# Mamba-2 SSD and a hard-swish MLP on one core: chunk 0's C load, the order of the opening and the weights' signs

## The chip, the cores and the metric

The kernel runs on one core of a Trainium2 chip. The metric is the device time in microseconds from launch to end, the median of several runs. Times inside a run are told on the clock of the profiled execution: 0 is the start of its span. Engines are PE (TensorE, with PEld for its weight loads), DVE (VectorE), ACT (ScalarE), POOL (GpSimd) and SP (SyncE, which here only issues DMAs); "ACTq" and "SPq" are DMA issues on the queues of ACT and SP.

## What is computed

A state-space scan in chunks, and then a two-layer MLP over all its tokens (the reference's own chunks have 32 tokens; the kernel takes 128, the same mathematics):

```
x: [4, 8, 768, 32]   a: [4, 8, 768]   B, C: [4, 8, 768, 16]
w_in: [256, 2048]    w_out: [2048, 256]        (both float64)

per batch and head, per chunk:
  cum     = cumsum(log a)
  M[i,j]  = (C_i . B_j) * exp(cum_i - cum_j)   for j <= i
  y_i     = sum_j M[i,j] x_j  +  exp(cum_i) * C_i . state
  state   = exp(cum_end) * state + sum_j exp(cum_end - cum_j) B_j x_j^T

X = y as [4 * 768 tokens, 8 * 32]
h = X @ w_in
out = (h * clip(h + 3, 0, 6) / 6) @ w_out
```

[...]

## The kernel before, in words

The 768 tokens are six chunks of 128. Chunk c has 4 batches x 128 tokens = 512 columns; chunk k's MLP is woven with chunk k + 1's scan. The order on every engine is written out by hand (a manual schedule): each engine runs its instructions in the order of the program text, and waits on semaphores for its operands. The order around the change is that of the main body from L969 on.

**Loads.** `load_bc` (L89) loads B and C of a chunk. Chunks 1 and 2 get them with tokens outermost; chunk 0's C, and C and B of chunks 3 to 5, are laid out by pairs of heads in `pairs_first` (L100): eight DMAs of 32 KB each, issued by SP (L104), one for each batch b and parity h, each from a source whose outermost dimension is 4 heads. Each DMA signals one of eight semaphores in turn, so the ninth waits until the first has landed, and so on; the first weights are the first in this round, `a` the second. Chunk 0's C comes after these two (with B, which ACT issues, among them), so that its sixth load waits for the first weights and its eighth for the first load of C. Behind C, SP issues x (L122) and the second part of the weights (L143).

**Weights.** `load_w(i)` (L132) loads one of eight parts of 1 MB: 0 to 3 are quarters of w_in's columns, 4 to 7 quarters of w_out's rows. Three raw buffers are there. `decode(i)` (L195) is a generator that is advanced by `weights(i, n)`, n steps at a time, so that its instructions lie where the main body puts them. Its steps for a part (128 x 1024 elements):

- ACT copies the top 16 bits of each double (L206).
- VectorE builds the significand in two instructions (L209, L213); VectorE cuts the exponent (L223) and the sign (L225) out of the 16 bits.
- ACT turns the exponent into the bits of a bfloat16 power of two by two relus (L229, L231), which also clip.
- VectorE joins the sign to it (L236) and multiplies it with the significand (L249). The result is a quarter of the first layer's weights (`first_in`), or of `w_out`.

**Chunk 0, the opening.** Decays: VectorE and ACT make cum of `a` (L277 to L293, in three bfloat16 parts), PE forms cum_i - cum_j in PSUM (`diff`, in two halves `diff_less` L364 and `diff_pick` L373, over a mask of L352), ACT takes the exponential (`diff_exp` L381). The same products for chunk 1 (`diff(1, ...)`) are also made here. POOL scales B by the decay to the end of a half chunk (`ends`, L412). PE turns B (`turn_b`, L438, copied by ACT at L447). VectorE turns C by 32 x 32 squares (`turn_squares` L481) and masks it by head parity (`part_heads` L488), POOL fades it (`fade` L494). `scores` (L543) is C.B, followed by `into_state` (L555); `multiply` (L585) multiplies decays and scores on VectorE; `mix` (L611) applies them to x and `from_state` (L516) adds the state's part; `keep` (L625) copies y to SBUF on ACT; `renew` (L594, L565) makes the new state. The second part of the scan over `a` (`add_up(ends_at[1])`, L282) feeds two stores by SP (`store_rows`, L299 and L301) and six transposes (`turn_cum` L329) whose result is negated and copied by VectorE (`by_token` L332). `busy` (L506) is a product of the identity with itself that nobody reads.

**First layer of chunk 0.** `mlp_in(0, f)` (L636) for f = 0 to 15: two products of 128 x 512 with f's weights, in four PSUM banks in turn; ACT (L715) and VectorE (L720) empty the bank of f into gT, so f + 4 waits for that. f = 0 to 3 use part 0 of the weights, 4 to 7 part 1, and so on. The steps of parts 2 to 5 are woven between them. The second layer (`first_out`, L735) follows and uses parts 4 to 7. From chunk 1 on the layers are done in another form (L684, L794, L861), with sums of weights and of gT.

Of the kernel before, what the change touches and what calls it, by code (L numbers as in the profile page):

```python
# [21 lines left out]
def kernel(  # L22
# [66 lines left out]
    def load_bc(c):  # L89

        sl = slice(c * P, (c + 1) * P)

        def tokens_first(src, queue=nc.sync, **where):
            t = loads.tile([P, NB * NH, N], FP32, **where)
            queue.dma_start(out=t, in_=src[:, :, sl, :].rearrange("b h s n -> s (b h) n"))
            return t

        def pairs_first(src):  # L100
            t = loads.tile([P, 2, NB, 4, N], FP32, name="pairs", tag="bc")
            for b in range(NB):
                for h in range(2):
                    nc.sync.dma_start(  # L104
                        out=t[:, h, b].rearrange("s a n -> s (a n)"),
                        in_=src[b, h:NH:2, sl, :].rearrange("h (s a) n -> h s (a n)", a=4))
# [25 lines left out]
    def load_w(i, queue=nc.sync):  # L132

        raw = loads.tile([P, NK * FP * 2 * P], U32, name="raw", bufs=NRAW)
        if i < NP:
            cols = slice(2 * i * FP * P, 2 * (i + 1) * FP * P)
            src = moe_w_in[:, cols].rearrange("(k p) f -> p k f", p=P)
            dst = raw.rearrange("p (k f) -> p k f", k=NK)
        else:
            r0 = (i - NP) * FP * P  # L140
            src = moe_w_out[r0:r0 + FP * P, :].rearrange("(k p) m -> p k m", p=P)
            dst = raw.rearrange("p (k m) -> p k m", k=FP)
        queue.dma_start(out=dst, in_=src)  # L143
        raws[i] = raw
# [1 line left out]
    load_w(0, nc.scalar)  # L146
    load_bc(0)
    load_x(0)
    load_w(1)
    nc.scalar.preload_act_table_set("natural_log_exp_and_others")  # L150


# [24 lines left out]
    half_up = const.tile([P, 1], FP32, name="half_up")  # L177
    nc.vector.memset(half_up, UP / 2)
    bias_hi = const.tile([P, 1], FP32, name="bias_hi")
    nc.vector.memset(bias_hi, 1151.0 * 2 ** 7)  # L180
    bias_lo = const.tile([P, 1], FP32, name="bias_lo")
    nc.vector.memset(bias_lo, 255.0 * 2 ** 7)
    head = const.tile([P, NQ, 2], FP32, name="head")
# [11 lines left out]
    def decode(i):  # L195

        n = NK * FP * P  # L200
        top = raws[i].bitcast(U16).rearrange("p (n w) -> p n w", w=4)[:, :, 3]
        lo, hi = (raws[i].rearrange("p (n w) -> p n w", w=2)[:, :, w] for w in range(2))
        se = att.tile([P, 2, n], U16, name="wse")
        s, e = se[:, 0], se[:, 1]
        m = att.tile([P, n], U32, name="wm")
        nc.scalar.copy(out=s, in_=top)  # L206

        def significand():
            nc.vector.tensor_scalar(  # L209
                out=m, in0=hi, scalar1=0xFFFFF, scalar2=0x100000,  # L210
                op0=ALU.bitwise_and, op1=ALU.bitwise_or)
            yield
            nc.vector.scalar_tensor_tensor(  # L213
                out=m.bitcast(FP32), in0=lo, scalar=2.0 ** -32, in1=m, op0=ALU.mult,
                op1=ALU.add)
# [16 lines left out]
        next(parts_m, None)  # L232
# [4 lines left out]
        m, e = m.bitcast(FP32), e.bitcast(BF16)  # L237
        if i < NP:
            if i < 2:
                dst = att.tile([P, NK, FP * P], FP32, name="w32", tag="y", bufs=3)  # L240
            else:
                dst = ffn.tile([P, NK, FP * P], FP32, name="w32", tag=("wide", "back")[i - 2])
            first_in[i] = dst
            m, e = (t.rearrange("p (k f) -> p k f", k=NK) for t in (m, e))
        else:
            dst = w_out[:, (i - NP) * FP:(i - NP + 1) * FP, :]
            m, e = (t.rearrange("p (k f) -> p k f", k=FP) for t in (m, e))
        unit = 2.0 ** -20 if i >= NP else 2.0 ** -20 / Z
        nc.vector.scalar_tensor_tensor(  # L249
            out=dst, in0=m, scalar=unit, in1=e, op0=ALU.mult, op1=ALU.mult)  # L250

# [77 lines left out]
            nc.tensor.transpose(out=c_ps[:, c], in_=cum_c[:, c], identity=ident[:G, :G])  # L329

    def by_token(c_ps):
        nc.vector.tensor_scalar(  # L332
            out=cum_n[:, 2:], in0=c_ps[:, 2:], scalar1=-1.0, scalar2=None, op0=ALU.mult)


    def y_tile(name, dtype):
# [163 lines left out]
        part_heads(c)  # L500
        fade(c)

    def busy(n, bank):

        for _ in range(n):
            nc.tensor.matmul(  # L506
                out=bank.rearrange("p (b i) -> p b i", b=NB), lhsT=ident,
                rhs=ident.unsqueeze(1).to_broadcast([P, NB, P]), start=True, stop=True)

    def from_state(c, a, pairs=range(NQ)):  # L510

        csT, state = bTs[c][2], (mids[c] if a else states[c - 1])
# [501 lines left out]
    renew(0)  # L1014
    weights(1, 1)
    load_eto(1)
# [151 lines left out]
```

## Time and profile before

| What | Value |
|---|---|
| Median of 3 runs | 345.14 us (345.08 to 348.86) |
| The profiled execution's own time | 345.45 us |
| Its span | 343.7 us |
| PE busy | 334.6 us, 97% |
| VectorE busy | 220.1 us, 64% |
| ACT busy | 173.2 us, 50% |
| POOL busy | 142.7 us, 42% |
| First-layer products of chunk 0 start (L636) | 22.98 us |
| They end, second layer of chunk 0 starts (L735) | 50.55 us |
| Chunk 0's C is turned (L481) | 12.63 us |
| Second weights' first pass on ACT (L206) | 18.95 us |

The page gives busy time by engine and, in 40 slices of the span, the busy share in tenths. In a timeline each row has the start, the length (of several instructions merged, from the first start to the last end), the engine, the line, the operation, output and input, and in brackets the idle time of the engine ahead of it with what ended it. The chain of waits is followed back from an end, each piece with start and length. In a table by stretches each row has a stretch, its length, the busy time of the five engines with the number of instructions, the granted TensorE clock, the DMA engines' share and the GB/s that they moved.

### The profile page before, as it was taken

How to read it: one execution, taken by the hardware profiler on the slowest of the kernel's cores; microseconds unless marked ns; L12 is line 12 of the kernel's file. 1: busy time of each engine (PE TensorE's matmuls, PEld its weight loads, DVE VectorE, ACT ScalarE, POOL GpSimd, SP SyncE). 2: the span in 40 equal slices, each digit the busy share in tenths (PEclk: the TensorE clock that was granted, in tenths of full speed). 3: DMA queues.
4: the chain of work that ended last, by engine and by line, in shares of the span. 5: the costliest groups of instructions: out<-in, count | busy, mean ns of one | idle time of the engine just before them, and what ended most of it. 6: DMA issues, size and time to landing. Idle time of an engine off the chain costs nothing.

```text
span 343.7 us, 8181 instructions
## 1 busy us (share of the span) xinstructions
PE 334.6 (97%) x3378; PEld 266.5 (78%) x3378; DVE 220.1 (64%) x357; ACT 173.2 (50%) x359; POOL 142.7 (42%) x139
## 2 busy tenths in 40 slices
PE   6889999999999999999999999999999999999996
PEld 2554448888778888888888888888887788888995
DVE  6689999999698647775438666447666324676011
ACT  4769878738874561564551564561564010565000
POOL 3300000093299923099611199610099400089500
PEclk9999999999999999999999999999999999999999
DMA  8888959206941057242029242051200010200010
GB/s 173 163 341 169 242 187 176 53 2 95 192 61 23 5 69 159 34 60 51 2 34 176 46 56 58 6 64 17 34 13 0 2 19 1 34 12 2 0 33 31
DMA packets 91605, 24.89 MB, mean 72 GB/s; under 512 B 84208, under 2 KB 87952, under 8 KB 91056
## 3 DMA queue, kind: packets, MB, share of 16 engines
q1 hardware_dynamic: 87184, 23.06, 34.8%
q10 hardware_dynamic: 4384, 1.31, 1.7%
q8 instruction: 26, 0.43, 0.5%
q14 instruction: 11, 0.09, 0.1%
HBM read 21.07 MB, written 3.29 MB: 71 GB/s over the span
## 4 chain that ended last, share of the span: by engine, by line
PE 75%; issue 11%; DMA 4%; DVE 2%; ACT 2%; POOL 2%; SPq 2%; POOLq 0%; DVEq 0%
PE h L684 31%; PE wb L861 13%; PE wc L861 8%; PE wa L861 8%; PE oa L794 4%; PE ob L794 4%; PE y L611 2%; PE y L516 2%; DMA raw<-in_moe_w_in_dram 2%; PE cb L543 2%; DMA eto<-cum_e 1%; ACT L L401 1%; POOL bs L412 1%; DMA pairs<-in_C_dram 1%; SPq L321 1%
## 5 line engine op out<-in xcount | busy, mean ns | idle before, releaser
L708 DVE SCALAR_TENSOR_TENSOR gT<-gT,h 128x512 f32<-128x512 f32 x80 | 54.9, 687 | 30.7 <-ACT gT L707 27.9
L707 ACT ACTIVATE gT<-h,half_up 128x512 f32<-128x512 f32 x80 | 55.1, 690 | 33.2 <-PE h L684 33.1
L780 POOL TENSOR_TENSOR s<-gT 128x512 f32<-128x512 f32 x20 | 25.8, 1288 | 66.4 <-DVE gT L708 66.4
L684 PE MATMUL h<-gap,w_gap 128*128 128x512 f32 x160 | 51.8, 409 | 0.0
L684 PE MATMUL h<-high,w_high 128*128 128x512 f32 x160 | 50.7, 398 | 0.1
L684 PE MATMUL h<-low,w_low 128*128 128x512 f32 x160 | 50.3, 395 | 0.0
L700 ACT ACTIVATE h<-h 128x512 f32<-128x512 f32 x40 | 23.5, 588 | 30.4 <-PE h L684 30.4
L684 PEld LDWEIGHTS h<-high,w_high 128*128 128x128 f32 x160 | 29.5, 188 | 8.5 <-DVE h L697 2.1
L684 PEld LDWEIGHTS h<-low,w_low 128*128 128x128 f32 x160 | 30.1, 188 | 7.2
L684 PEld LDWEIGHTS h<-gap,w_gap 128*128 128x128 f32 x160 | 29.9, 188 | 7.1 <-DVE gap L678 0.5
L401 ACT ACTIVATE L<-L,cum_n 128x64 f32<-128x64 f32 x128 | 31.6, 337 | 0.7 <-POOL L L162 0.7
L861 PE MATMUL wb<-s,w_out 128*128 128x256 f32 x128 | 30.7, 382 | 0.0
L419 POOL TENSOR_TENSOR tmp<-state,eto 128x256 f32<-128x256 f32 x5 | 3.6, 721 | 61.0 <-ACT eto L405 60.9
L735 PE MATMUL o<-w_out,gT 128*128 128x256 f32 x128 | 28.7, 381 | 0.0
L697 DVE TENSOR_SCALAR h<-h 128x512 f32<-128x512 f32 x40 | 27.7, 692 | 1.2 <-PE h L684 1.2
L636 PE MATMUL h<-yT,w 128*128 128x512 f32 x64 | 27.7, 594 | 0.0
L780 POOL TENSOR_TENSOR s<-s,gT 128x512 f32<-128x512 f32 x20 | 26.9, 1345 | 1.6
L585 DVE TENSOR_TENSOR L<-L,cb 128x512 f32<-128x512 f32 x24 | 15.3, 682 | 19.1 <-PE cb L543 16.3
L735 PEld LDWEIGHTS o<-w_out,gT 128*128 128x128 f32 x128 | 24.1, 190 | 3.8 <-issue 0.5
L861 PEld LDWEIGHTS wb<-s,w_out 128*128 128x128 f32 x128 | 24.0, 190 | 3.6
L412 POOL TENSOR_TENSOR bs<-B,L 128x128 f32<-128x128 f32 x24 | 13.7, 584 | 30.9 <-ACT L L401 25.8
L780 POOL TENSOR_TENSOR gT<-gT 128x512 f32<-128x512 f32 x20 | 25.9, 1294 | 0.0
(141 smaller groups left out, 534.3 us busy)
## 6 DMA issues: line engine op xcount, KB each, us to landing
raw<-in_moe_w_out_dram SPq DMA_DIRECT2D x4, 1024.0 KB
L<-cum_d SPq DMA_DIRECT2D x8, 512.0 KB
xt<-in_x_dram SPq DMA_DIRECT2D x6, 512.0 KB
raw<-in_moe_w_in_dram SPq DMA_DIRECT2D x3, 1024.0 KB
out_dram<-back SPq DMA_DIRECT2D x128, 16.0 KB
eto<-cum_e SPq DMA_DIRECT2D x20, 64.0 KB
B<-in_B_dram SPq DMA_DIRECT2D x5, 256.0 KB
raw<-in_moe_w_in_dram ACTq DMA_DIRECT2D x1, 1024.0 KB
```

The costliest lines, as they stand in the source:

```text
L401: nc.scalar.activation(Ls[c][:, b, h], Ls[c][:, b, h], AF.Exp, bias=cum_n[:, c, g:g + 1])
L412: nc.gpsimd.tensor_tensor(out=bss[c][:, hs], in0=Bs[c][:, hs], in1=Ls[c][:, b, :, HT - 1:HT].to_broadcast([P, NH, N]), op=ALU.mult)
L636: nc.tensor.matmul(out=h.rearrange("p r i -> p (r i)"), lhsT=first_in[f // FP][:, j, f % FP * P:(f % FP + 1) * P], rhs=yTs[k][:, j], start ...
L684: nc.tensor.matmul(out=h, lhsT=w[:, j, f * P:(f + 1) * P], rhs=y[:, j], start=(start and j == 0), stop=True, skip_group_check=True)
L697: nc.vector.tensor_scalar(out=h, in0=h, scalar1=-Z / UP, scalar2=None, op0=ALU.mult)
L700: nc.scalar.mul(h, h, -Z / UP)
L707: nc.scalar.activation(g, h, AF.Relu, bias=half_up, scale=UP * UP / 6.0)
L708: nc.vector.scalar_tensor_tensor(out=g, in0=g, scalar=UP, in1=h, op0=ALU.min, op1=ALU.mult)
L735: nc.tensor.matmul(out=o[:, b % 2], lhsT=gTs[0][:, f, b * P:(b + 1) * P], rhs=w_out[:, f], start=(f == 0 and b % 2 == 0), stop=True, skip_ ...
L780: nc.gpsimd.tensor_tensor(out=o, in0=p_, in1=q_, op=op)
L794: nc.tensor.matmul(out=bank[:, slot], lhsT=lhs[:, j], rhs=rhs[:, j], start=(clear and j == 0), stop=True, skip_group_check=True)
L861: nc.tensor.matmul(out=bank[:, slot], lhsT=lhs[:, j], rhs=rhs[:, j], start=(clear and j == 0), stop=True, skip_group_check=True)
```

## The change

- `pairs_first` issues one DMA for each pair of heads q and parity h, all batches in it, into 32 partitions; the outermost dimension on both sides is 32 rows.
- In the opening, B is turned and chunk 1's differences 2 and 3 are made before POOL's `ends`; chunk 1's differences 0 and 1 are made one before and one after `scores`; `mix` and `keep` are done by halves with `turn_cum` and `by_token` between them; `by_token` runs on ACT; the two calls of `busy` are gone.
- `load_w(1)` moves from behind x to behind `store_rows`, ahead of `load_w(2)`; `load_w(3)` moves behind `by_token`.
- In `decode`, ACT takes the absolute value of the top 16 bits (read as bfloat16) instead of copying them, so the exponent needs no cutting; the scales and biases of the two relus are changed to fit. For parts 0 to 5 one VectorE instruction takes the sign out of the raw words and joins it (L250 of the changed kernel, `and` then `or`); it replaces three (L223, L225, L236). For parts 6 and 7 ACT makes the sign as a bfloat16 of 1 or -1 (L228) and VectorE multiplies it in (L248). Part 0 joins and multiplies in two halves of its columns.

```diff
@@ load_bc: pairs_first
-            for b in range(NB):
+            for q in range(NQ):
                 for h in range(2):
                     nc.sync.dma_start(
-                        out=t[:, h, b].rearrange("s a n -> s (a n)"),
-                        in_=src[b, h:NH:2, sl, :].rearrange("h (s a) n -> h s (a n)", a=4))
+                        out=t[32 * q:32 * q + 32, h].rearrange("s b a n -> s b (a n)"),
+                        in_=src[:, 2 * q + h, sl, :].rearrange("b (s a) n -> s b (a n)", a=4))
@@
     load_x(0)
-    load_w(1)
@@
-    nc.vector.memset(bias_hi, 1151.0 * 2 ** 7)
+    nc.vector.memset(bias_hi, 1151.0 + 7.5 / 16)
@@ decode
-        nc.scalar.copy(out=s, in_=top)
+        signed = i >= NP + 2
+        nc.scalar.activation(e.bitcast(BF16), top.bitcast(BF16), AF.Abs)
...
-        if i == 0:
+        if i < 2:
             next(parts_m)
             next(parts_m)
         yield
-        nc.vector.tensor_scalar(
-            out=e, in0=s, scalar1=0x7FF0, scalar2=None, op0=ALU.bitwise_and)
-        nc.vector.tensor_scalar(
-            out=s, in0=s, scalar1=0x8000, scalar2=None, op0=ALU.bitwise_and)
+        nc.scalar.activation(e, e, AF.Relu, bias=bias_hi, scale=-1.0 / 16)
         next(parts_m, None)
         yield
-        nc.scalar.activation(e.bitcast(BF16), e, AF.Relu, bias=bias_hi, scale=-8.0)
-        yield
-        nc.scalar.activation(e, e.bitcast(BF16), AF.Relu, bias=bias_lo, scale=-1.0)
+        nc.scalar.activation(e, e, AF.Relu, bias=bias_lo, scale=-128.0)
+        if signed:
+            nc.scalar.activation(s.bitcast(BF16), top.bitcast(BF16), AF.Sign)
         next(parts_m, None)
-        if i and i + NRAW < 2 * NP:
-            load_w(i + NRAW)
-        yield
-        nc.vector.tensor_tensor(out=e, in0=e, in1=s, op=ALU.bitwise_or)
+        yield
...
-        nc.vector.scalar_tensor_tensor(
-            out=dst, in0=m, scalar=unit, in1=e, op0=ALU.mult, op1=ALU.mult)
+        wide = dst.shape[-1]
+        for cols in ((slice(0, wide // 2), slice(wide // 2, wide)) if i == 0 else (slice(0, wide),)):
+            mc, ec, sc, tc_, out_ = (t[:, :, cols] for t in (m, e, s, top, dst))
+            if signed:
+                nc.vector.tensor_tensor(out=ec, in0=ec, in1=sc, op=ALU.mult)
+            else:
+                nc.vector.scalar_tensor_tensor(
+                    out=ec.bitcast(U16), in0=tc_, scalar=0x8000, in1=ec.bitcast(U16),
+                    op0=ALU.bitwise_and, op1=ALU.bitwise_or)
+            if i and i + NRAW < 2 * NP:
+                load_w(i + NRAW)
+            if i:
+                yield
+            nc.vector.scalar_tensor_tensor(
+                out=out_, in0=mc, scalar=unit, in1=ec, op0=ALU.mult, op1=ALU.mult)
@@ by_token
-        nc.vector.tensor_scalar(
-            out=cum_n[:, 2:], in0=c_ps[:, 2:], scalar1=-1.0, scalar2=None, op0=ALU.mult)
+        nc.scalar.mul(cum_n[:, 2:], c_ps[:, 2:], -1.0)
@@ keep
-    def keep(c):
-        yTs[c] = y_tile("yT", FP32)
-        for u in range(2):
-            for a in range(2):
-                nc.scalar.copy(out=y_half(yTs[c], a, u), in_=ys[c][a, u])
+    def keep(c, u):
+        for a in range(2):
+            nc.scalar.copy(out=y_half(yTs[c], a, u), in_=ys[c][a, u])
@@ the main body, opening
     diff(0, 2, 3)
-    weights(0, 1)
+    weights(0, 2)
     for b in range(NB):
         diff_exp(0, b)
     first_eto()
+    turn_b(0)
     diff(1, 2, 3)
-    weights(0, 1)
-    for b in range(NB):
-        ends(0, b)
-    turn_b(0)
-    diff(1, 0, 1)
-    busy(1, ps.tile([P, NB * P], FP32, name="d", tag="f0"))
-    weights(0, 1)
     diff_exp(1, 2)
     diff_exp(1, 3)
     turn_squares(bcs[0][0], turned(0)[2])
     part_heads(0)
-    fade(0, HALF[1], nc.gpsimd)
+    for b in range(NB):
+        ends(0, b)
     add_up(ends_at[1])
     store_rows()
+    load_w(1)
     load_w(2)
     weights(0, 1)
+    diff(1, 0)
+    fade(0, HALF[1], nc.gpsimd)
     scores(0)
+    diff(1, 1)
     multiply(0)
+    yTs[0] = y_tile("yT", FP32)
+    mix(0, (0,))
+    keep(0, 0)
+    c_ps = ps.tile([P, NC, G], FP32, name="c_ps", tag="f3")
+    turn_cum(c_ps)
+    by_token(c_ps)
+    weights(0, 1)
     load_w(3)
-    c_ps = ps.tile([P, NC, G], FP32, name="c_ps", tag="f1")
-    turn_cum(c_ps)
-    busy(1, ps.tile([P, NB * P], FP32, name="d", tag="f0"))
-    weights(0, 1)
-    weights(1, 1)
-    by_token(c_ps)
-    mix(0)
-    keep(0)
-    weights(1, 3)
+    mix(0, (1,))
+    keep(0, 1)
+    weights(1, 4)
     renew(0)
     weights(1, 1)
```

More of the change, by code (lines that the diff above doesn't have):

```diff
@@ L222, in decode @@
         yield
-        nc.vector.tensor_scalar(
-            out=e, in0=s, scalar1=0x7FF0, scalar2=None, op0=ALU.bitwise_and)
-        nc.vector.tensor_scalar(
-            out=s, in0=s, scalar1=0x8000, scalar2=None, op0=ALU.bitwise_and)
+        nc.scalar.activation(e, e, AF.Relu, bias=bias_hi, scale=-1.0 / 16)
         next(parts_m, None)
         yield
-        nc.scalar.activation(e.bitcast(BF16), e, AF.Relu, bias=bias_hi, scale=-8.0)
+        nc.scalar.activation(e, e, AF.Relu, bias=bias_lo, scale=-128.0)
+        if signed:
+            nc.scalar.activation(s.bitcast(BF16), top.bitcast(BF16), AF.Sign)
+        next(parts_m, None)
         yield
-        nc.scalar.activation(e, e.bitcast(BF16), AF.Relu, bias=bias_lo, scale=-1.0)
-        next(parts_m, None)
-        if i and i + NRAW < 2 * NP:
-            load_w(i + NRAW)
-        yield
-        nc.vector.tensor_tensor(out=e, in0=e, in1=s, op=ALU.bitwise_or)
-        m, e = m.bitcast(FP32), e.bitcast(BF16)
+        m, e, s = m.bitcast(FP32), e.bitcast(BF16), s.bitcast(BF16)
         if i < NP:
@@ L243, in decode @@
             first_in[i] = dst
-            m, e = (t.rearrange("p (k f) -> p k f", k=NK) for t in (m, e))
+            parted = NK
         else:
             dst = w_out[:, (i - NP) * FP:(i - NP + 1) * FP, :]
-            m, e = (t.rearrange("p (k f) -> p k f", k=FP) for t in (m, e))
+            parted = FP
+        m, e, s, top = (t.rearrange("p (k f) -> p k f", k=parted) for t in (m, e, s, top))
         unit = 2.0 ** -20 if i >= NP else 2.0 ** -20 / Z
-        nc.vector.scalar_tensor_tensor(
-            out=dst, in0=m, scalar=unit, in1=e, op0=ALU.mult, op1=ALU.mult)
+        wide = dst.shape[-1]
[13 more added lines that the diff above has]
+                out=out_, in0=mc, scalar=unit, in1=ec, op0=ALU.mult, op1=ALU.mult)
     pick = const.tile([P, G], BF16, name="pick")
@@ L501, in turn_all @@
         fade(c)
[L503 to L508, printed above, removed]
     def from_state(c, a, pairs=range(NQ)):
```

## The prediction

> **What bounds the kernel now.** First the page's head and its slices. The span is 343.7 us; the profiled run took 345.45 us, 1.75 more for what lies around it, and the median of the three runs shown is 345.14.
>
> ```profile
> PE   6889999999999999999999999999999999999996
> DVE  6689999999698647775438666447666324676011
> PEclk9999999999999999999999999999999999999999
> DMA  8888959206941057242029242051200010200010
> ```
>
> A slice is 8.6 us. PE is short of full only in the first three slices and the last; asked by stages it is busy 27.57 of the 27.57 us from 22.98 to 50.55, and 255.29 of the 258.7 us after 85. So what can be won lies ahead of 22.98, where the first product of the first layer (L636) starts, and only as far as the products behind it then run without a hole. Next the chain of waits, for the time before that:
>
> ```profile
> 0.80 5.92 DMA raw<-in_moe_w_in_dram
> 6.74 0.61 SPq L104
> 7.40 1.23 SPq L104
> 8.67 3.78 DMA pairs<-in_C_dram
> 12.63 1.18 DVE csT L481
> 14.86 1.25 PE cb L543 x61
> 19.80 0.93 issue
> ```
>
> The reader sees a queue, not an engine: SP's sixth load of C starts when the first weights have landed (6.73), the eighth at 8.67, and its 32 KB take 3.78 us more. VectorE has nothing from 10.29 to 12.63. The stretches by time show how C moves:
>
> ```profile
> 8.00:10.00 2.00, 2.00 (x71) 1.40 (x71) 1.93 (x4) 1.35 (x3) 0.00 (x0) 1.00 0.36 54
> 20.00:23.00 3.00, 2.26 (x101) 1.94 (x101) 2.93 (x6) 1.23 (x4) 0.00 (x0) 1.00 1.04 425
> ```
>
> The last two columns are the DMA engines' share and GB/s: while C is awaited only 0.36 of the 16 engines work, at 54 GB/s; later loads get 425. Last the timelines, for what follows L636 and for single durations:
>
> ```profile
> 18.95 1.17 ACT L206 COPY wse<-raw 128x1024 uint16<-128x1024 uint16 x1 [1.16 <-DMA raw<-in_moe_w_in_dram]
> 26.46 1.23 DVE L249 SCALAR_TENSOR_TENSOR w<-wm,wse 128x1024 f32<-128x1024 f32 x1
> 8.26 1.23 DVE L213 SCALAR_TENSOR_TENSOR wm<-raw,wm 128x1024 f32<-128x1024 uint32 x1
> 2.14 3.57 PE L352 MATMUL d<-hide,ident_h 128*128 128x512 bf16 x8 [2.14 <-POOL head L184]
> 7.56 0.60 PE L364 MATMUL d<-less,split 128*128 128x512 bf16 x2 [1.00 <-DVE split L293]
> 23.39 0.37 SPq L143 DMA_DIRECT2D raw<-in_moe_w_out_dram x1
> ```
>
> The 16 columns f of the first layer take 27.57/16 = 1.72 us each. f = 4 needs the second part of the weights; it is done at 27.69, and PE asks for it at 22.98 + 4 x 1.72 = 29.87. So an earlier start has 2.2 us of slack there, and no more.
>
> **The change, part by part.** Times are on the span's clock.
>
> *C with 32 rows outermost.* Same eight loads of 128 pieces of 256 bytes, same order on SP. The sixth still waits for the first weights, 6.74; the seventh starts at 7.40 and takes between 0.53 (the usual issue of such a load, later chunks) and 1.23; the eighth starts at 8.0 to 8.65. From there its landing took 3.78 with a third of the engines. If all take part there is no backlog, and what remains is a load's latency: the x load issued at 9.27 shows as rising traffic in the half microsecond from 10.5, 1.2 to 1.7 later, and some 0.5 for the end. I take 2.2 (bounds 1.6 and 3.78): C is there at 10.4, bounds 9.6 (VectorE's own work on the first weights ends 9.49) and 12.63. The share of 0.36 is why I lean to the low end. [...] For the C and B of chunks 3 to 5 the same edit is worth nothing: L481 waited for pairs once in the run.
>
> *VectorE behind it.* Transpose to cT takes 1.20, the two cT 0.80, the scan until SP stores 1.23 (12.63, 13.83, 14.63, 15.86). From 10.4: cT ready 12.4, scan done 13.63. The two bit operations of weight part 0 (0.42 and 0.43) are gone from here; they lay in the idle time, worth nothing. ACT takes part 0's first relu (1.15) ahead of the four exponentials, which start at 8.95 instead of 8.57; PE and ACT then finish bT near 12.0, before cT, so that costs nothing unless C is earlier than 9.6.
>
> *PE.* Without the idle products (1.12 each; the first lay in the wait for cT, the second ahead of L611) and with half of chunk 1's differences moved behind the scores, PE is through its earlier products at 12.5: the last of chunk 1's differences ended at 12.87, half a bank pair (0.6) has gone, and the later exponentials free a bank some 0.25 later. Scores start at 12.55 (before 14.86), end 13.75; into_state 0.86, the moved difference 0.6: 15.2. Mix of the first half 0.85 (L585 for its heads ends 15.0), from_state 0.61, c_ps 0.43, second half 0.79, 0.61: 18.5. First-layer products start about 18.6, 4.4 earlier. VectorE's L585 ends 16.2; the joined signs and the product of part 0, by halves, are four times 0.69: first half 17.5, all by 18.9, f = 2 needs it at 22 (L250 and L257 by halves, priced by L585's 0.68 for 512 columns). by_token moves to an idle ACT (0.28). The copies of y end at 19.1.
>
> *Second weights later.* load_w(1) moves on SP from behind x (10.04, held there 4.08, landed 18.95) to behind both stores, and these wait for the scan. Before, SP went from store to next weights in 0.87 (15.86 to 16.73): now 13.63 + 0.87 = 14.5, then load_w(2) at once; load_w(3) waits for part 0's joining, about 18.2 (before 17.3). The w_out load behind it waits for part 1's joining, 24.1 (before 23.39), and what SP has queued after that, chunk 1's decays, C, B and x, comes 0.7 later; POOL asks for the decays at 67.9 and PE for C and B at 66, so 35 us cover it. A megabyte on a drained queue: the w_out load issued at 23.39 shows 240 to 400 GB/s from 25.0 to about 28.2, 4.8 from issue; the first one took 5.92 in company, the one of 17.3 about 7 behind two others. I take 4.8: landed 19.3, 0.35 later than before although all around it is over 2 us earlier. That is now the tight place. Queued behind it: ACT's three passes, 1.15, 1.19 and 1.19 with gaps: 22.85. VectorE: the joined signs. The trace has no such 16-bit operation with a strided input; 0.68 (L236) and 1.23 (L213, same stride in bytes) bound it, I take 1.22: 24.1. Then L594 and L565, 1.0, and the product 1.22: 26.3. Behind these stands the first evacuation, 0.68, which frees f = 4's bank: 27.0. PE itself would be there at 18.6 + 6.89 = 25.5, so it stands 1.5 us at f = 4.
>
> *After that.* VectorE's work per part was 4 x 0.60 + 4.40 = 6.8 against PE's 6.89; it becomes 4 x 0.60 + 4.1 = 6.5. f = 8 asks at 33.9 and gets part 2 at 33.5, f = 12 has 0.8 to spare. Parts 6 and 7 give ACT one pass more each (2 x 1.1), covered by ACT's idle 2.0 before bT (66.73) and the earlier start. From there everything shifts alike.
>
> The sum: 29.87 - 27.0 = 2.9 us. Span 340.8, profiled run 342.55; against the median, which is 0.3 lower, 342.2.
>
> **The rivals.**
>
> *C is no faster.* For it: the sixth load still waits for 6.73, and B's small packets share the engines. Against it: 0.36. Then the transpose stays at 12.63, the weights are issued at 16.73 and land at 21.5, f = 4 at 29.2: 0.7 won, 344.4.
>
> *PE's stop stays.* The 0.93 us at 19.80 waited for nothing the profile shows, while the DMA carried about 400 GB/s. If it falls into the same place of the program, ACT's copies end at 20.0 and hold its first pass: f = 4 at 27.75, 2.1 won, 343.0. Against it: at that place the weights are then only starting.
>
> *Weights in time.* If C lands at 9.6 and the joined signs take 0.68, f = 4 would be free at 25.6, about PE's own 25.5; 4.3 won, 340.8. That is the floor: PE's own chain does not get shorter.
>
> *PE at half speed (slower).* The trace has two speeds: the eight products at 2.14 stand 0.43 apart, the same shape at 7.56 takes 0.60 for two, though PEclk says 1.00 for both. Without the idle products PE could fall back. If all from the scores on (6.0 us to 18.6) ran at half speed, the first layer would start at 24.6 and f = 4 at 31.5: 1.6 lost, 346.8. It decides from 4.4 us lost on PE (1.5 slack and 2.9). Against it: after 7.5 the new order leaves PE fewer holes than the old, which had two of 0.9 and one of 0.6 and kept its speed. [...]
>
> **How the numbers follow.** The forecast's chain 0.55, C no faster 0.13, the stop stays 0.13, weights in time 0.11, half speed 0.05, something unseen 0.03. The likeliest gives 342.2; its own range is 341.4 (C at 9.6) to 343.2 (C a microsecond later than 10.4). With the rivals but the slow one: 340.7 to 344.9. About 2% (6.9 us) is what a measurement of this kernel tells from no change: only half speed for longer, or something unseen, goes beyond it. Faster 0.02, same 0.95, slower 0.03.
>
> **What would show it.** The DMA share between 6.5 and 10 above 1 and the transpose at about 10.4; L636 at about 18.6; the second weights' first ACT pass at about 19.3, waiting for the DMA; a hole of about 1.5 us on PE at f = 4, the wait put down to VectorE, and no further one up to the second layer; the joined signs near 1.22. Wrong it would be if the transpose still starts after 12, if the weights land after 20.5 or before 18, if VectorE falls behind at f = 8, or if products after 7.5 are 0.43 apart in the 16-bit shape.

## The result, and the profile after

The changed kernel takes 349.56 us (median of 18 runs, 346.59 to 351.74), the kernel before beside it 345.45 (18 runs, 344.84 to 348.86). The ratio is 1.0108, 95% interval 1.0085 to 1.0131: some 1.1% slower, within the 2% the prediction named, but on the wrong side and outside its range. The profiled execution took 351.21 us with a span of 349.3, so 1.9 lie around the span (before 1.75). Ratios here are formed without disturbed runs, so they need not equal the quotient of the medians.

Each run also has its mean granted PE clock, and the spans go with it. Of the 18 runs after, 2 have 0.995 (spans 344.7 and 345.7), 9 about 0.990 (346.7 to 348.2) and 7 about 0.985 (348.2 to 349.9); none is at full clock. The profiled run is one of the 0.984. First its slices of 8.7 us:

```profile
span 349.3 us, 8168 instructions
PE   6859999999999999999999999999999999999996
PEclk9967999999999999999999999999999999999999
DMA  9783999601981009234009425014110000200000
```

The row PEclk was 9 throughout before; now its third and fourth slices read 6 and 7, and PE's third slice 5 instead of 8. The loss lies between 17 and 35 us. The chain of waits gives the place:

```profile
7.33 0.43 SPq L104
7.80 3.25 DMA pairs<-in_C_dram
11.23 1.13 DVE csT L488
13.41 1.20 PE cb L543 x59
14.95 0.76 issue
17.87 0.25 PE y L516 x3
18.12 3.89 issue
22.02 1.01 PE y L516 x8
25.74 30.20 PE h L634 x64
```

C is there at 11.23 instead of 12.63, the scores start 1.45 earlier. Then PE stops twice for "issue", a wait for nothing that the profile shows: 0.76 us, and 3.89 us at 18.12, in the middle of one and the same line (3 products of L516 before, 13 after). Behind it the first layer starts at 25.7, not at 22.98, and takes 30.2 us instead of 27.6. The stretches by time say why (last columns: granted clock, DMA engines' share, GB/s):

```profile
0.00:18.13 18.13, 13.39 (x349) 7.64 (x349) 12.96 (x30) 10.49 (x19) 5.79 (x18) 1.00 0.87 147
8.00:10.00 2.00, 2.00 (x69) 1.29 (x67) 1.56 (x2) 1.97 (x4) 0.00 (x0) 1.00 0.96 115
18.00:20.00 2.00, 0.12 (x3) 0.00 (x0) 1.76 (x3) 0.27 (x1) 0.00 (x0) 1.00 0.98 393
20.00:22.00 2.00, 0.00 (x0) 0.00 (x0) 0.14 (x1) 0.00 (x0) 0.00 (x0) 0.64 1.00 403
24.00:26.00 2.00, 2.00 (x65) 1.72 (x50) 0.00 (x0) 0.58 (x2) 0.00 (x0) 0.50 0.61 240
28.00:30.00 2.00, 2.00 (x3) 0.67 (x2) 0.43 (x1) 1.97 (x3) 0.00 (x0) 0.50 0.00 0
30.00:32.00 2.00, 2.00 (x5) 0.91 (x4) 1.96 (x5) 1.25 (x3) 0.00 (x0) 0.80 0.13 9
```

While PE stands, the second and third parts of the weights (asked for at 15.26 and 15.78) pass at 400 GB/s; some 2.5 us after the stop began the clock falls to 0.50 and stays there for about 10 us (0.64 in 20 to 22, 0.80 in 30 to 32), during which first-layer products are twice as long (592 ns at the least, 1222 at the most). From the first layer's end on nothing differs: 293.35 us from there to the end, 293.15 before.

The stop can be counted. The first row above says that PE had run 349 products and 349 weight loads when it stopped; the same count for the kernel before, up to its own unexplained stop of 0.93 us at 19.80:

```profile
0.00:19.81 19.81, 15.12 (x350) 8.12 (x350) 14.00 (x32) 11.32 (x19) 5.80 (x18) 1.00 0.88 194
```

350 and 350. Two programs with a different order stop at the same count, once in the mix and once in L516; with PE's few other records (7 after, 5 before) it is behind the 705th record in both. The smaller stop of after, at 14.95, comes behind the 449th, 256 earlier. And the page has a queue for it (packets, megabytes, share of the engines' time), first for the whole run, then in the DMA view for 19.5 to 19.7 alone:

```profile
q8 instruction: 26, 0.43, 0.5%
```

```profile
q8 instruction: 1, 0.02, 31.2%
```

26 transfers of some 16 KB in the whole run, one of them in the middle of PE's stop, and none that starts from 13 to 19.5. They fit PE alone: 26 pieces of 256 are 6656 instructions, and by the page PE runs 3374 products and 3374 weight loads, VectorE 342 instructions and ScalarE 362. So the theory to test was: PE runs through its small products faster than its instructions come, 256 at a time; the piece behind the 705th record is asked for when PE enters the piece before it (15.71; an inference, since the trace shows when a transfer starts, here 19.6, and not when it was asked for), and here it queues behind the weights asked for from 15.26 on. The rivals: the later second weights cost by coming late ("late data"), or PE lost its clock because the two idle products are gone ("no idle products").

### The profile page after: what moved, and what is told of

Same layout as the page of the kernel before. It is cut to its first block, busy times and chain, and to the rows that moved or that the text cites. A ratio compares the mean times of both kernels' runs of the same rounds, so it can differ in the third digit from the quotient of the medians.

```text
span 349.3 us, 8168 instructions
## 1 busy us (share of the span) xinstructions
PE 337.0 (96%) x3374; PEld 268.4 (77%) x3374; DVE 216.3 (62%) x342; ACT 175.5 (50%) x362; POOL 142.1 (41%) x139
## 4 chain that ended last, share of the span: by engine, by line
PE 92%; DMA 3%; issue 2%; DVE 1%; ACT 1%; SPq 0%; DVEq 0%
PE h L682 31%; PE wb L859 12%; PE h L634 9%; PE wc L859 8%; PE o L733 8%; PE wa L859 8%; PE oa L792 4%; PE ob L792 4%; PE y L611 3%; PE y L516 2%; PE cb L543 2%; DMA raw<-in_moe_w_in_dram 2%; PE y L555 1%; DMA pairs<-in_C_dram 1%; PE t_ps L445 1%
## 5 line engine op out<-in xcount | busy, mean ns | idle before, releaser
L778 POOL TENSOR_TENSOR s<-gT 128x512 f32<-128x512 f32 x20 | 25.8, 1288 | 66.5 <-DVE gT L706 66.5
L634 PE MATMUL h<-yT,w 128*128 128x512 f32 x64 | 30.3, 637 | 0.0
L695 DVE TENSOR_SCALAR h<-h 128x512 f32<-128x512 f32 x40 | 27.6, 691 | 1.2 <-PE h L682 1.2
L634 PEld LDWEIGHTS h<-yT,w 128*128 128x128 f32 x64 | 13.0, 205 | 16.5 <-issue 14.5
```

What stands on the lines that cost most here:

```text
L634: nc.tensor.matmul(out=h.rearrange("p r i -> p (r i)"), lhsT=first_in[f // FP][:, j, f % FP * P:(f % FP + 1) * P], rhs=yTs[k][:, j], start ...
L695: nc.vector.tensor_scalar(out=h, in0=h, scalar1=-Z / UP, scalar2=None, op0=ALU.mult)
L778: nc.gpsimd.tensor_tensor(out=o, in0=p_, in1=q_, op=op)
```

## The experiments

All ran against the kernel before; a table of them stands at the end of this part. Line numbers are those of each kernel, and differ by up to 8 from those of the kernel that it varies. The first four vary the changed kernel.

**e1: the first of the second weights back in its old place.**

```
     load_x(0)
+    load_w(1)
...
     store_rows()
-    load_w(1)
     load_w(2)
```

> The changed kernel with load_w(1) back in its old place behind the x load, nothing else. Theory (the 3.89 us in which PE waits for nothing the profile shows, at its 698th to 705th instruction, is a fetch of its next instructions, held by the two megabytes of weights that are asked for at 15.3 and 15.6; the clock then falls to half for about 10 us): one megabyte less in the way, so the stop shrinks to between 0.9 and 2.5 us at the same count of instructions, the clock stays full from 20 to 30, 343 to 346 us. Rival 'late data' (what costs is that the second weights come later): the stop has nothing to do with the weights and stays at 3.9 us; the time changes by no more than the wait at f = 4, of which the changed kernel has none, so 349 to 350. Rival 'no idle products' (PE without them falls to half speed): half speed from 20 to 30 as before, 347 to 351.

Measured: 350.02 us (349.13 to 350.91), ratio 1.0130 (1.0085 to 1.0176). The stop is still 3.62 us and the clock 0.985 to 0.990. That refutes "late data", since part 1's weights are in time here, but the size of mine missed too. The edit takes less out of the way than I meant: part 1, asked for at 8.64, is still passing when PE enters the piece before at 15.62 (the DMA engines' share is 0.96 from 14 to 16), and part 2 was asked for at 15.19.

**e2: both idle products back.**

```
+    busy(1, ps.tile([P, NB * P], FP32, name="d", tag="f0"))
     scores(0)
...
+    busy(1, ps.tile([P, NB * P], FP32, name="d", tag="f0"))
     mix(0, (0,))
```

> The changed kernel with the two idle products back, one ahead of chunk 0's scores and one ahead of its mix, nothing else. Rival 'no idle products': PE keeps full speed, 344 to 346 us. Theory: the stop is found at the same count of instructions (16 of them are now taken by the idle products, so it lies up to 16 earlier in the program) and is still 3 to 4 us long; half speed for 7 to 10 us behind it; 348 to 351. Rival 'late data': 349 to 351, no difference.

(`busy` is the function of the kernel before. In the trace an idle product is two products and two weight loads, four records and not the eight instructions that I counted.)

Measured: 349.75 us (346.40 to 351.78), ratio 1.0080 (1.0040 to 1.0121). Two of the ten runs are at full clock, the profiled one among them, and in it the stop at the 705th record is 1.34 us; four of the ten have 0.985. The profile puts this stop down to ScalarE's copy of y (L630), but that had ended 0.93 us before. The idle products alone don't bring the time back, against that rival; and the profiled stop isn't 3 to 4 us, against mine: how long the fetch is held is not the same in every kernel that has the weights late. What stop the runs at a lower clock had is not known, since only one run has a profile.

**e3: 64 instructions more, early, in PE's wait for the scan.**

```
+    for _ in range(32):
+        nc.tensor.matmul(
+            out=ds[0, 0][:, 0], lhsT=ident_h, rhs=hide, start=True, stop=True)
     for b in range(2):
         mask_again(0, b)
```

> The changed kernel with 32 small products (64 columns, bf16, 64 instructions with their weight loads) put in at about 6.6 us, where PE waits for the scan, nothing else; they are overwritten. Theory: the stop is a matter of the count of instructions. It is found after 690 to 710 of them again, but 64 earlier in the program: no longer in L516 behind the first half of the mix, but inside the mix, L611. Its length is 1 to 3.9 us, as the fetch before it is asked for about 1.3 us sooner, and still meets the weights. Both rivals and any cause that lies in the data: the stop stays in L516, where a product waits for its operand, and its length stays 3.9. Time by the theory 344 to 350, by the rivals 349 to 350.

Measured: 349.25 us (348.83 to 350.86), ratio 1.0117 (1.0072 to 1.0161). PE's waits (line, what ended the wait, us in all, times, longest), then the counts up to the two stops:

```profile
PE y L516 <- issue: 3.2, 1, 3.2
PE y L611 <- issue: 1.8, 1, 1.8
```

```profile
0.00:16.63 16.63, 13.90 (x349) 8.97 (x350) 11.42 (x28) 10.40 (x18) 5.78 (x18) 1.00 0.92 146
0.00:21.26 21.26, 16.71 (x477) 11.34 (x477) 14.60 (x32) 11.77 (x22) 5.78 (x18) 1.00 0.91 184
```

The stop left its place in L516 behind the first half of the mix and went into the mix itself, L611, 64 instructions earlier in the program and at the same count, 699; and a second stop, which the changed kernel has nowhere, appears 255 instructions later at 954, in the second L516. (With the few other records these are 705 and 961, 256 apart.) What these products read comes from where it came before. The stops belong to the count. This settles what kind of wait it is.

**e4: no weights asked for between 9 and 19.**

```
     load_x(0)
+    load_w(1)
...
     store_rows()
-    load_w(1)
-    load_w(2)
...
     keep(0, 0)
+    load_w(2, nc.scalar)
```

> The changed kernel with load_w(1) in its old place behind the x load, and load_w(2) issued on ScalarE's queue behind the first half's two copies of y, so that no weights are asked for between 10 and about 18.5. Theory: with nothing large in the way the fetch that PE waits for at its 700th instruction takes its quiet time: a stop of 0 to 1 us, full clock throughout, the first product of the first layer at 19 to 20.5, 340.5 to 343.5 us. Rival 'late data': parts 1 and 2 are in time in any case, so it is like e1. Rival 'no idle products': half speed comes back somewhere between 12 and 30, 346 or more.

Measured: 346.82 us (346.15 to 348.41), ratio 1.0044 (1.0019 to 1.0070); two of ten runs at full clock (spans 344.2 and 344.6), three at 0.995, five at 0.990. The stretches of the stop, and the fetch in the DMA answer for 16.8 to 16.9:

```profile
16.00:18.00 2.00, 2.00 (x114) 1.50 (x94) 1.97 (x4) 1.04 (x4) 0.00 (x0) 1.00 0.35 99
18.00:20.00 2.00, 0.85 (x20) 0.70 (x17) 1.97 (x4) 0.34 (x2) 0.00 (x0) 1.00 0.00 0
```

```profile
q8 instruction: 1, 0.02, 60.9%
```

With no weights asked for since 8.70 the fetch starts some 2.8 us earlier, though PE entered the piece before at the same time (15.68, after 15.71), and the stop is 1.15 instead of 3.89; in both PE goes on 2.4 us after the fetch starts. The DMA engines were not at rest yet when PE entered that piece: part 1 was passing until about 16.5 (share 0.91 from 16.0 to 16.5, 0.38 in the next half microsecond). The first layer starts at 21.5. So the mechanism holds, but 340.5 to 343.5 did not come: two stops of 0.74 and 1.15 remain with this order of loads, the clock still falls by a step or two in most runs, and the first layer waits 0.8 and 0.3 us for VectorE.

The next four took two parts of the change alone, on the kernel before, and improved on e4.

**e5: before, without its two idle products.** Edit: the two `busy(1, ...)` lines go.

> The kernel before without its two idle products, nothing else. Theory (PE's small products run faster than their instructions are fetched, 256 at a time; an empty PE then costs granted clock): the stop at the 705th record stays in sight and takes in the second idle product's 1.07 us, so it grows from 0.93 to about 2.0 and the first product of the first layer comes within 0.4 us of 22.98; nothing is won. With two holes of 1.9 and 2.0 us more runs lose one or two steps of clock (0.995, 0.990), 344.5 to 348. Rival 'no idle products' in its strict form (they alone keep the clock): every run has 0.990 or less, 347 to 350. If they are dead weight: 1 us is won, 344.3.

Measured: 350.11 us (349.51 to 351.22), ratio 1.0113 (1.0059 to 1.0167), all four runs at 0.990. PE's waits from 12 to 23:

```profile
PE y L516 <- issue: 2.8, 1, 2.8
PE y L555 <- issue: 0.5, 1, 0.5
```

The strict form of the rival is right here: leaving out two products of 1.07 us whose result nobody reads costs 1.1%. By the trace it is through the same stop: PE reaches the 705th record at 18.91 instead of 19.81, waits 2.8 there, and the first layer starts at 24.9 and at half clock. PE goes on 1.0 later than before (21.7 after 20.7), as it also enters the piece before 0.8 later (16.77 after 15.99, behind the stop of 0.5); in this profile PE's products also ran at a lower rate up to about 11 (see the last section), so it is open how much of that comes from the idle products. I had the place right, the price too low.

**e6: before, with C by heads and nothing else.**

```
-            for b in range(NB):
+            for q in range(NQ):
                 for h in range(2):
                     nc.sync.dma_start(
-                        out=t[:, h, b].rearrange("s a n -> s (a n)"),
-                        in_=src[b, h:NH:2, sl, :].rearrange("h (s a) n -> h s (a n)", a=4))
+                        out=t[32 * q:32 * q + 32, h].rearrange("s b a n -> s b (a n)"),
+                        in_=src[:, 2 * q + h, sl, :].rearrange("b (s a) n -> s b (a n)", a=4))
```

> The kernel before with chunk 0's C loaded by heads, 32 rows outermost, nothing else. Theory: the transpose of C starts at 10.8 to 11.3 instead of 12.63, the scores at 13.9 (PE's earlier products end there) instead of 14.76; the second weights are asked for 1.2 to 1.5 us earlier and meet the fetch for the 705th record, whose stop grows from 0.93 to between 1.5 and 3; the first layer starts between 22.3 and 23.8, 343.5 to 347.5 us, not faster than before by more than 1. Rivals: without that stop 0.8 us are won at once, 344.7.

Measured: 349.32 us (348.33 to 350.48), ratio 1.0096 (1.0071 to 1.0121), clock 0.995 or 0.990 in all ten runs. The chain, and the stretches:

```profile
7.73 0.60 PE d L364 x2
18.29 0.86 PE y L611 x52
19.15 3.04 issue
24.93 7.39 PE h L636 x14
```

```profile
20.00:22.00 2.00, 0.00 (x0) 0.00 (x0) 1.93 (x4) 0.00 (x0) 0.00 (x0) 1.00 0.93 377
24.00:26.00 2.00, 2.00 (x18) 1.37 (x17) 0.00 (x0) 1.32 (x3) 0.00 (x0) 0.50 0.82 255
```

The faster load alone makes the kernel slower by as much as the whole change. It ends VectorE's scan earlier, so SP asks for the third and fourth parts of the weights at 15.10 instead of 16.73, and these now pass ahead of PE's fetch: the stop of before, at the same record and in the same line, grows from 0.93 to 3.04. The time is beyond the 347.5 that I gave as its upper end.

**e7: e4, with the second weights' decode brought forward.**

```
     multiply(0)
+    load_w(2, nc.scalar)
+    weights(0, 1)
+    load_w(3)
+    weights(1, 2)
     yTs[0] = y_tile("yT", FP32)
     mix(0, (0,))
     keep(0, 0)
-    load_w(2, nc.scalar)
...
-    weights(0, 1)
-    load_w(3)
...
-    weights(1, 4)
+    weights(1, 2)
```

> As the run that held the weights back (load_w(1) early, load_w(2) on ScalarE's queue), but load_w(2) right behind the four exponential and state operations, and two of part 1's three ScalarE passes ahead of the copies of y. Theory: the stops stay at about 0.75 and 1.15, the first layer starts at 21.3 to 22, and the two waits of 0.8 and 0.3 us in the first layer are gone; at full clock the span is 342 to 343.3, and most runs have 0.99 to 1.0: 344 to 346 us. If the second weights' earlier request meets the fetch again: a stop of 2 to 3 us and 346 to 349.

Measured: 347.50 us (345.32 to 348.58), ratio 1.0032 (0.9999 to 1.0064). The waits in the first layer are gone, as expected, but one run of ten is at full clock (span 343.6); five have 0.995, four 0.990. So 344 to 346 did not come. In the profiled run, which has 0.995, the longest stop is 1.42 us, with one of 0.2 ahead of it.

**e8: e7 with the two idle products.** Edit: as in e2, on e7.

> As the run beside it (weights held back, part 1 decoded early), with the two idle products back, one ahead of the scores and one ahead of the mix. Theory: PE waits for instructions there in any case (0.64 and 0.75 us around the scores, 1.15 behind the mix), and an idle product is 1.07 us of work in 8 instructions; the stops shrink by what the products fill, so the first layer starts no more than 0.6 us later than without them, and the clock stays at 1.0 in most runs: 343.5 to 345. If the idle products are dead weight: 1 to 2 us longer than without them.

Measured: 344.95 us (344.63 to 345.21), ratio 0.9962 (0.9933 to 0.9991); ten of ten runs at full clock. The chain:

```profile
20.08 0.68 PE y L517 x16
22.52 27.66 PE h L642 x64
```

The idle products delay the first layer by 0.4 us against e7 (22.4 for 22.0) and win 2.5. The stops are 0.34 and 1.06; the second begins at the 705th record, here a wait for a semaphore that ScalarE had raised at 17.3, and the profile puts it down to the next thing that ScalarE ended, a pass that PE reads nothing of. The kernel is faster than the one before by 0.4% (within those 2%), and by the medians 1.3% faster than the changed one.

Of the last four, three go back to the kernel before.

**e9: before, with C by heads and the weights held.** Edit: as in e6, and

```
     store_rows()
-    load_w(2)
...
-    load_w(3)
...
     weights(1, 1)
+    load_w(2, nc.scalar)
+    load_w(3, nc.scalar)
     by_token(c_ps)
```

> The kernel before with chunk 0's C loaded by heads, and load_w(2) and load_w(3) issued on ScalarE's queue behind its first pass of part 1 (about 18 to 20 us) instead of on SP at 15.1; the two idle products stay. Theory (with C alone changed, what cost 3.5 us was that the second weights, asked for at 15.1, met the fetch that PE needs at its 705th record, 3.04 us of stop): the stop shrinks to 0.5 to 1.3, the clock stays at 1.0 in most runs, the first product of the first layer starts at 21.5 to 22.6, and 343.5 to 345 us come out, faster than before by up to 2. Rival (C's new load itself disturbs PE, or an earlier scan does): 347 to 350 as with C alone.

Measured: 344.51 us (344.18 to 345.32), ratio 0.9964 (0.9940 to 0.9987); ten of ten at full clock. No stop is left at the 705th record. The chain, and one stretch:

```profile
7.69 1.03 PE d L364 x2
15.50 1.24 PE cb L543 x59
22.80 27.66 PE h L636 x64
```

```profile
16.00:18.00 2.00, 1.48 (x112) 1.15 (x95) 1.25 (x3) 1.44 (x3) 0.00 (x0) 1.00 0.38 106
```

C's load did no harm by itself: against e6 only two issues have moved (later, and to ScalarE's queue), and by the medians 4.8 us are won. Here the fetch starts at 17.34, 0.7 after PE entered the piece before (16.63), and the weights are asked for only at 17.96. The median is the lowest here.

**e10: before, with only the weights held.** Edit: e9's second part alone.

> The kernel before with load_w(2) and load_w(3) issued on ScalarE's queue behind its first pass of part 1, nothing else. Theory: the stop of 0.93 us at 19.80 was the fetch behind these loads, so it shrinks to 0.5 or less or goes; 344 to 345.5 us, no run or few below a clock of 1.0. Rival: the stop has another cause and stays at 0.93; the time stays, 345.5 to 346.

Measured: 345.59 us (344.84 to 347.18), ratio 0.9993 (0.9964 to 1.0021). The stop of before shrinks as the theory has it; the half microsecond that this is worth can't be told from no change:

```profile
PE y L611 <- issue: 0.5, 1, 0.5
```

What C's load wins on top of it can't be told either: the intervals of e9 and e10 overlap.

**e11: the changed kernel, the stop filled with idle products.** Edit: as in e2, with `busy(4, ...)` ahead of the mix.

> The changed kernel with one idle product back ahead of the scores and four, one behind the other, ahead of the mix (4.3 us of work in 32 instructions), nothing else: PE works while its next instructions are fetched. Theory: the stop falls to under 1 us, since the fetch arrives at about 21 to 22 whatever PE does; the first layer starts at 23 to 24.5, but at full clock: the clock is 1.0 in most runs, 344.5 to 346.5 us, so the price of the stop in the changed kernel was mostly the clock behind it. Rival (the stop is waited out behind the idle products too, or the clock falls for another cause): 349 to 353.

Measured: 349.52 us (348.99 to 349.76), ratio 1.0113 (1.0090 to 1.0136), four of four runs at full clock.

```profile
PE y L618 <- issue: 0.7, 1, 0.7
```

The stop is 0.7 and the clock is kept, both as the theory said, yet nothing is won: PE goes on at 22.87, the first layer starts at 25.5 and waits 0.8 more. So my claim that the stop's price was mostly the clock behind it falls. A late fetch costs its time with the clock kept, too (PE goes on at 19.24 in e4); the clock comes on top where PE stands empty. How much of the delay here is the idle products' own work this run can't tell: PE enters the piece before at 16.2 instead of 15.7 (in this profile its products also ran at a lower rate up to about 11, see the last section), and the fetch starts at 20.6 instead of 19.6.

**e12: before, with the second weights later and nothing else.** Edit: `load_w(1)` from behind `load_x(0)` to behind `store_rows()`.

> The kernel before with load_w(1) moved behind the two stores, nothing else, so that it is asked for at 16.7 with load_w(2); old C, old decode, idle products. Theory: as the scan ends late here, the fetch for the 705th record (asked for at about 16) is ahead of the weights; the stop stays near 0.9 and the clock at 1.0. Part 1 lands at 21 to 22.5, three ScalarE passes and VectorE's part follow, so PE waits 0 to 2.5 us at f = 4: 345 to 348. Rival 'late data' (that the second weights come later is what costs in the change): 347 to 350 here too. If the fetch is held as in the changed kernel: a stop of 2 to 4 and 348 to 351.

Measured: 349.38 us (348.12 to 350.56), ratio 1.0113 (1.0082 to 1.0145), clock 0.995 to 0.989. There is no stop at the 705th record: the scan ends late here, and the fetch was ahead of the weights, as expected (PE entered the piece before at 15.82, the fetch starts at 16.70; the weights were asked for at 16.55). But PE's waits and ScalarE's timeline show another hole:

```profile
PE h L635 <- ACT yT L624: 3.1, 1, 3.1
```

```profile
23.44 1.09 ACT L205 COPY wse<-raw 128x1024 uint16<-128x1024 uint16 x1 [5.83 <-DMA raw<-in_moe_w_in_dram]
24.43 1.19 ACT L624 COPY yT<-y 128x256 f32<-128x256 f32 x4
```

In the order of before, ScalarE's first pass of part 1 stands ahead of the copies of y, so PE waits for the weights through ScalarE. That is the rival "late data" in this order, by a wait I had not seen; the changed kernel has the copies first and is free of it. The clock falls behind this hole as behind the others (0.50 from about 25.8 to 29.2), so what counts is that PE is empty, not why.

**In sum** (times in us; clock steps: runs at 1.000 / 0.995 / 0.990 / 0.985 of the mean granted clock, rounded):

```
kernel                            median  ratio (95%)              PE's hole     first layer  clock steps
changed                           349.56  1.0108 (1.0085, 1.0131)  0.76 + 3.89   25.7         0/2/9/7
 e1 first of second weights back  350.02  1.0130 (1.0085, 1.0176)  0.75 + 3.62   25.3         0/0/3/1
 e2 idle products back            349.75  1.0080 (1.0040, 1.0121)  0.20 + 1.34   22.6         2/3/1/4
 e3 64 instructions more          349.25  1.0117 (1.0072, 1.0161)  1.82 + 3.21   24.7         0/3/1/0
 e4 weights held                  346.82  1.0044 (1.0019, 1.0070)  0.74 + 1.15   21.5         2/3/5/0
 e7 held, decode earlier          347.50  1.0032 (0.9999, 1.0064)  0.19 + 1.42   22.0         1/5/4/0
 e8 e7 + idle products            344.95  0.9962 (0.9933, 0.9991)  0.34 + 1.06   22.4         10/0/0/0
 e11 stop filled                  349.52  1.0113 (1.0090, 1.0136)  0.73          25.5         4/0/0/0
before                            345.45                           0.93          23.0         49/9/5/0
 e5 no idle products              350.11  1.0113 (1.0059, 1.0167)  0.45 + 2.81   24.9         0/0/4/0
 e6 C by heads                    349.32  1.0096 (1.0071, 1.0121)  3.04          24.9         0/4/6/0
 e12 second weights later         349.38  1.0113 (1.0082, 1.0145)  3.13 (ACT)    25.1         0/3/1/0
 e9 C by heads, weights held      344.51  0.9964 (0.9940, 0.9987)  none          22.7         10/0/0/0
 e10 weights held                 345.59  0.9993 (0.9964, 1.0021)  0.45          22.5         9/1/0/0
```

Holes and starts are those of the profiled run, the clock that of all runs (for the kernel before, of its 63 beside e1 to e12). Waits for data of under 1 us are not among the holes.

The traces show the same parts in every stop behind the 705th record: in all twelve profiles that have one, PE goes on 2.2 to 2.8 us after the transfer of 16 KB starts (18.5 in the kernel before, 19.6 in the changed one, 16.8 in e4, 19.4 in e6, 17.9 in e10). What differs is how long that transfer takes to start once PE has entered the piece before: 0.7 and 0.9 us in e9 and e12, where the DMA engines had little or nothing to move, 1.2 in e4, 2.5 in the kernel before, 3.7 to 4.3 in e1, e6, e11 and the changed kernel.

## Why the prediction was wrong, point by point

**What bounds the kernel now** held: all that was lost lies ahead of the first layer and in its first third.

**C** held in kind. The share between 8 and 10 is 0.96 instead of 0.36, so about 15 engines of 16 where it was 6, and 115 GB/s instead of 54, with x in the later figures, which was asked for at 8.28 instead of 9.27. The transpose starts 1.4 us earlier. That all the engines would take part in C was my estimate; the runs show the share of all that passes and not C's own part. My 2.2 for the last landing was 3.25 (the bounds were 1.6 to 3.78), so 11.23 instead of 10.4; the 0.5 for a load's end in it is a term that no run shows.

**VectorE, the weights' signs and their prices** held: the joined signs take 1.23 (forecast 1.22) and 0.68 by halves.

**Second weights later** was mis-sized: asked for at 15.26 (14.5) and, with a second megabyte at once, 6.6 instead of 4.8 to landing, so 21.9 instead of 19.3. It set nothing, since PE was later still: ScalarE began at 26.06, behind its copies of y, and f = 4 never waited for a bank.

**PE: "First-layer products start about 18.6"** is the step that failed. They start at 25.7. Of the 7.1 us, 0.86 come from C, 0.76 and 3.89 from two stops, and some 1.3 from half clock between 22.02 and 25.74 (e4 needs 2.4 us for the same work at full clock, against 3.7); these make 6.8. Another 2.6 were lost in the first layer at half clock. I summed products' durations and had no term for the instructions themselves; but 256 of these instructions take PE about 2.4 us (15.71 to 18.12), and in e4 the next 256 are ready only 3.6 us after PE enters the piece (15.68 to 19.24), in the changed kernel 6.3 (15.71 to 22.02). With the DMA engines idle it would be some 3.2, an estimate from the 0.7 to 0.9 of e9 and e12 and the 2.4 behind it; no run shows a stop under these conditions. So the chain of durations left out a limit that holds with little in the way, too: e4 starts at 21.5.

**"PE's stop stays"** named the right thing and dismissed it for the wrong reason: "at that place the weights are then only starting". The stop does not wait for a place in the program but for a count, and weights that are only starting were the worst of the cases here: the weights were asked for at 15.26 and 15.78, PE entered the piece before at 15.71, and the fetch started at 19.6. I gave it 0.93 us and a chance of 0.13; it was 3.89.

**"PE at half speed (slower)"** was the rival with the right sign, with a chance of 0.05. That the new order leaves PE fewer holes than the old was true of the waits for data (behind the scan one of 0.7, where there were 0.9 and 0.6), and false with the stops (0.76 and 3.89, where there was 0.93). Of an empty PE behind the scores' start the profiles show: every one with a hole of 2.8 to 3.9 us lost clock, one of 1.42 with 0.2 ahead of it did in e7, and 1.34 in e2, 1.15 in e4 and 1.06 in e8 did not. So the runs give no length from which the clock falls. And the idle products, which I priced as 1.12 us each of dead work, are what keeps the kernel before at full clock in most runs (49 of 63, none of 4 in e5).

**After that** held: from the first layer's end on the two kernels agree to 0.2 us.

What stays open: why the same kernel loses one step in one run and three in the next (e2), and the 0.25 us more around the span, which most runs of the kernels with the new decode show and the others don't. No run was made with the new decode alone.

## What to carry to other kernels

Count PE's instructions where its products are small: a stop that waits for nothing in the profile, at the same instruction count in two versions (705) and again 256 further, was an instruction fetch here, and a bulk load that passed ahead of it made it longer (0.93 us before, 3.04 in e6). A faster load or an earlier scan can therefore lose time by bringing the bulk load forward; hold that load until the fetch has passed (e6 against e9: two issues moved, 4.8 us). Before removing work that looks idle, look at what keeps the clock: here each of three edits, each cheap by its own sum, cost 1% alone through a hole of about 3 us in PE (2.81 in e5, 3.04 in e6, 3.13 in e12).

## What the hardware showed beside

Half clock lasted about 3.4 us in e6, e7 and e12 (one step each), 6.8 in e5 (two) and 10.2 in the profiled run after (three), so pieces of some 3.4. One piece is 1.7 us lost, 0.005 of the run's mean clock; that is what separates the groups of spans, 343.8, 345.5 and 347.2 for the kernel before (medians).

The row PEclk doesn't show every slow phase. Two products of 128x512 at 7.7 take 0.60 us in e6 and 1.03 in e9 (the chains shown above), both with PEclk 1.00; in e5, e7, e9 and e11 the profiled run kept this lower rate until about 11. In e9 it cost 1.3 us on the way to the scores (15.50 against 14.21 in e6).
